# Loading the first feed-forward weights in two halves of 64 rows, with an activation tile between them

## The chip, the cores and the metric

One core of one Trainium2 chip. The metric is device time in microseconds (us) of one execution. Times inside a profile count from the start of its span, which is some 1.8 us shorter than the timed execution.

## The reference

The kernel computes a layer norm, then attention and a gated feed-forward network on the normalised input, and multiplies the two:

```python
x  = A_x                              # 1 x 2048 x 448, bf16
xn = layernorm(x)
s  = attention(xn, k_cache[last 512], v_cache[last 512], wq, wo)   # 16 heads of 256, 8 kv heads
g  = silu((gelu(xn @ w_gate) * (xn @ w_up)) @ w_down)              # w_gate, w_up: 448 x 1792
out = x + s * g
```

Only the first 10 us matter here. There the kernel loads x in tiles of 128 rows (called x0, x1, x2, x3 below), normalises and transposes them, and starts the gate and up products.

## The kernel before

The width 448 is three blocks of 128 rows of weights (k = 0, 1, 2) and a remainder of 64 rows. TensorE runs products of 64 rows in pairs, one on array rows 0 to 63, one on rows 64 to 127. In phase 0 the gate product takes the lower rows and the up product the upper ones; in phase 1 they change places.

```python
def group(units, lo, hi, start, stop, phases=(0, 1)):
    for p in phases:
        ph, part = p if isinstance(p, tuple) else (p, None)
        ks = {None: [2, 1, 0, NK], 0: [2, 1], 1: [0, NK]}[part]     # NK: the remainder rows, phase 0 only
        ...
            for u, j in ((0, ph), (1, 1 - ph)):                     # u: row half, j: 0 gate, 1 up
                rows = slice(R * u, R * u + R)                      # R = 64
        ...
        o = mms(lst, reads + rr + xb, b_ps[b:b + 2], before)        # waits for what it reads

load_x("sp", 0, 1)          # x0 on SyncE's queue (SP)
load_x("act", 1, 1)         # x1 on ScalarE's queue (ACT)
load_w("sp", 0, 0)          # gate, block 0: 128 rows x 3 k x 384 columns, 288 KB
load_w("act", 0, 1)         # up, block 0
load_x("sp", 2, 1)          # x2
load_wr("sp", 0, 0)         # remainder rows, 48 KB each
load_wr("act", 0, 1)
load_x("act", 3, 1)         # x3
...
act(tmp[:, 1, 0:1], epst[:, :], ACT.Sqrt, ...)   # brings ScalarE's table in, behind its four issues
load_x("sp", 4, 2)
for i in (1, 2):            # blocks 1 and 2, all on SP
    load_w("sp", i, 0); load_w("sp", i, 1); load_wr("sp", i, 0); load_wr("sp", i, 1)
```

The order of the engines' work in the head matters too. In every trace here VectorE and ScalarE run their instructions in the order in which the program lists them:

```python
ln_first(0); ln_first(1)              # statistics (VectorE), deviation (ScalarE)
ln_second(0)                          # reciprocal, normalise (VectorE)
ln_tp_pe(0, ((0, 6), (1, 4)))         # transposes on TensorE, copies on ScalarE
ln_second(1, "act")
ln_first(2)                           # statistics of x2: its deviation stands ahead of ...
gu_group(HEAD, PH, (0, 1), ((0, 0),)) # tile 0: phase 0, k = 2 and 1
ln_tp_pe(1, T)                        # ... the copy of the transposed tile 1 on ScalarE
gu_group(HEAD, PH, (0, 1), ((0, 1), 1))
ln_bn(3)                              # statistics of x3, ahead of tile 2's normalisation
ln_second(2)
ln_aggr(3); ln_std_act(3); ln_second(3)
gu_group(HEAD[:2], PH[:2], (1, 2), (0,))
ln_tp_pe(2, T)
...
```

The softmax here doesn't subtract the row's maximum and nothing guards it: scores larger than these inputs give would overflow.

## Time and profile before

| | before |
|---|---|
| time, first 3 runs | 556.67 us (556.21 to 556.74) |
| span of the profiled execution | 554.7 us |
| TensorE (PE) busy | 547.6 us, 99% |
| chain of waits on PE | 98% |

From the page of the kernel before: its first line, PE's busy time, and the chain that ended last.

```profile
span 554.7 us, 9719 instructions
PE 547.6 (99%) x3603; PEld 261.2 (47%) x3628; DVE 317.2 (57%) x817; ACT 273.6 (49%) x727; POOL 32.7 (6%) x64
...
PE 98%; DMA 1%; issue 0%; DVE 0%; SPq 0%; ACT 0%
```

The chain in order of time, kernel before (start us, us, what):

```profile
1.65 4.66 DMA x<-in_A_x_dram
6.34 0.64 DVE stats L375
7.00 0.19 DVE mv L378
7.22 0.29 ACT ve L391
7.51 0.49 ACT xnT L322
8.14 0.62 PE bank L328 x16
...
10.18 116.23 PE bank L328 x1028
```

The last thing that TensorE ever waits long for is x2: its load, its statistics, its deviation, and behind the deviation, on the same engine, a copy that belongs to tile 1. After 10.18 us the chain is matmuls almost to the end. The timeline of the same kernel (start us, us, engine, line, what, and in brackets the idle time before it and its releaser):

```profile
1.18 0.42 SPq L316 DMA_DIRECT2D wgu<-in_B_w_gate_dram  x1
1.65 0.48 SPq L316 DMA_DIRECT2D x<-in_A_x_dram  x1
2.89 1.28 ACT L322 ACT_TABLE_LOAD   x1 [2.89 <-issue]
6.34 0.63 DVE L375 BATCH_NORM_STATS2 stats<-x 128x6 f32<-128x448 bf16 x1 [0.30 <-DMA x<-in_A_x_dram]
8.14 0.34 PE L328 MATMUL bank<-xnT,wgu 64*128 64x128 bf16 x6 [0.37 <-ACT xnT L322]
```

When a load is complete is read below from the semaphore events in the trace: each load adds 16 increments, and the time of the last one is quoted.

### The profile page before, as it was taken

How to read it: one execution, taken by the hardware profiler on the slowest of the kernel's cores; microseconds unless marked ns; L12 is line 12 of the kernel's file. 1: busy time of each engine (PE TensorE's matmuls, PEld its weight loads, DVE VectorE, ACT ScalarE, POOL GpSimd, SP SyncE). 2: the span in 40 equal slices, each digit the busy share in tenths (PEclk: the TensorE clock that was granted, in tenths of full speed). 3: DMA queues.
4: the chain of work that ended last, by engine and by line, in shares of the span. 5: the costliest groups of instructions: out<-in, count | busy, mean ns of one | idle time of the engine just before them, and what ended most of it. 6: DMA issues, size and time to landing. Idle time of an engine off the chain costs nothing.

```text
span 554.7 us, 9719 instructions
## 1 busy us (share of the span) xinstructions
PE 547.6 (99%) x3603; PEld 261.2 (47%) x3628; DVE 317.2 (57%) x817; ACT 273.6 (49%) x727; POOL 32.7 (6%) x64
## 2 busy tenths in 40 slices
PE   8999999999999999999999999999999999999997
PEld 5554444444544444554444444544444454444455
DVE  6673734443385588326588745258747625858722
ACT  5432324353485588205588635058747505758600
POOL 1120580000000000000000000000000000000000
PEclk9999999999999999999999999999999999999999
DMA  9540399901156077413086803157704713618601
GB/s 295 115 141 9 79 302 307 213 1 39 38 134 96 5 149 157 88 35 92 1 153 152 153 1 77 33 94 164 146 11 95 134 34 90 153 19 153 153 8 34
DMA packets 163599, 57.63 MB, mean 104 GB/s; under 512 B 151456, under 2 KB 160672, under 8 KB 163552
## 3 DMA queue, kind: packets, MB, share of 16 engines
q1 hardware_dynamic: 159488, 45.16, 38.8%
q0 software_dynamic: 3296, 11.27, 6.7%
q8 instruction: 29, 0.48, 0.4%
q10 hardware_dynamic: 768, 0.57, 0.3%
q14 instruction: 18, 0.15, 0.1%
HBM read 17.92 MB, written 1.84 MB: 36 GB/s over the span
## 4 chain that ended last, share of the span: by engine, by line
PE 98%; DMA 1%; issue 0%; DVE 0%; SPq 0%; ACT 0%
PE bank L328 98%; DMA x<-in_A_x_dram 1%; SPq L316 0%; DVE stats L375 0%; ACT xnT L322 0%; DVE tmp L681 0%; ACT ve L391 0%; DVE ofin L684 0%; PE bank L426 0%; DVE mv L378 0%
## 5 line engine op out<-in xcount | busy, mean ns | idle before, releaser
L643 ACT ACTIVATE p<-bank 128x512 f32<-128x512 f32 x256 | 149.2, 597 | 103.3 <-PE bank L328 101.4
L647 DVE TENSOR_SCALAR pn<-p,rden 128x512 bf16<-128x512 f32 x256 | 124.6, 487 | 14.4 <-DMA pT<-pn 5.4
L328 PE MATMUL bank<-pT,va 128*128 128x512 bf16 x512 | 120.8, 379 | 0.0
L328 PE MATMUL bank<-kT,qT 128*128 128x512 bf16 x487 | 117.8, 379 | 2.0 <-ACT qT L322 1.0
L328 PE MATMUL bank<-wo,oT 128*128 128x448 bf16 (+2 forms) x544 | 97.7, 341 | 0.0
L328 PE MATMUL bank<-xnT,wq 64*128 64x512 bf16 x768 | 94.4, 376 | 0.0
L328 PE MATMUL bank<-xnT,wgu 64*128 64x512 bf16 (+2 forms) x768 | 83.9, 350 | 0.4 <-ACT xnT L322 0.4
L328 PEld LDWEIGHTS bank<-pT,va 128*128 128x128 bf16 x512 | 50.1, 98 | 60.4 <-DMA pT<-pn 0.2
L328 PEld LDWEIGHTS bank<-kT,qT 128*128 128x128 bf16 x512 | 49.6, 98 | 61.3 <-issue 2.5
L328 PEld LDWEIGHTS bank<-wo,oT 128*128 128x128 bf16 x544 | 52.0, 98 | 45.5
L630 DVE CAST qT<-bank 128x512 bf16<-128x512 f32 x64 | 42.9, 692 | 51.9 <-PE bank L328 51.9
L322 ACT ACTIVATE qT<-bank 128x512 bf16<-128x512 f32 x64 | 38.2, 597 | 60.7 <-PE bank L328 59.1
L328 PEld LDWEIGHTS bank<-xnT,wq 64*128 64x128 bf16 x768 | 36.9, 94 | 46.5 <-ACT p L643 2.1
L322 ACT ACTIVATE gl<-bank 128x512 bf16<-128x512 f32 x56 | 33.2, 597 | 49.4 <-PE bank L328 46.2
L494 DVE TENSOR_TENSOR actT<-bank,gl 128x512 bf16<-128x512 f32 x56 | 37.8, 689 | 33.4 <-PE bank L328 26.6
L328 PEld LDWEIGHTS bank<-xnT,wgu 64*128 64x128 bf16 x768 | 36.9, 94 | 37.4 <-issue 0.7
L643 ACT ACTIVATION_READ_ACCUMULATOR p<-bank 128x1 f32 x256 | 52.8, 206 | 0.0
L646 DVE RECIPROCAL rden<-rsum 128x1 f32<-128x1 f32 x256 | 40.4, 158 | 20.6 <-ACT p L643 20.0
L681 DVE SCALAR_TENSOR_TENSOR tmp<-bank,g 128x448 f32<-128x448 f32 (+2 forms) x17 | 10.1, 597 | 72.5 <-PE bank L328 72.5
L666 DVE CAST oT<-bank 128x512 bf16<-128x512 f32 x64 | 43.8, 684 | 6.9 <-PE bank L328 6.9
L328 PE MATMUL bank<-wd,actT 128*128 128x448 bf16 x224 | 43.0, 353 | 0.0
L322 ACT ACTIVATE oT<-bank 128x512 bf16<-128x512 f32 x64 | 39.1, 611 | 7.0 <-PE bank L328 7.0
(39 smaller groups left out, 182.9 us busy)
## 6 DMA issues: line engine op xcount, KB each, us to landing
wo<-in_A_wo_dram POOLq DMA_DIRECT2D x4, 896.0 KB, 19.0
wq<-in_A_wq_dram POOLq DMA_DIRECT2D x2, 1536.0 KB, 10.0
va<-in_A_v_cache_dram POOLq DMA_DIRECT2D x8, 256.0 KB, 13.9
pT<-pn SPq DMA_TRANSPOSE x128, 2.8
xr<-in_A_x_dram POOLq DMA_DIRECT2D x16, 112.0 KB, 2.3
out_dram<-ofin SPq DMA_DIRECT2D x15, 112.0 KB, 1.7
wd<-in_B_w_down_dram SPq DMA_DIRECT2D x1, 1568.0 KB, 7.6
x<-in_A_x_dram SPq DMA_DIRECT2D x2, 448.0 KB, 4.4
```

What stands on the lines that cost most here:

```text
L322: K.op("act", lambda e, o=o, i=i: e.activation(o, i, func, scale=scale), reads, writes)
L328: ins = e.matmul(o, lhsT=l, rhs=r, start=st, stop=sp)
L494: K.op("dve", lambda e: e.tensor_tensor(actT[:, c % 2, f, :], bank[b + 1], gl[:, s, :], ALU.mult), (b_ps[b + 1], b_gl[s]), (b_actT[c % 2][ ...
L630: K.op("dve", lambda v, s=s, b=b: v.tensor_copy(qT[:, s, 1, :], bank[b + 1]), (b_ps[b + 1],), (b_qT[s][1],))
L643: K.op("act", lambda e, b=b, r=r, z=z: e.activation(p32[:, z, :], bank[b], ACT.Exp, scale=att_scale, accum_out=rsum[:, r:r + 1]), (b_ps[b] ...
L646: K.op("dve", lambda e, r=r: e.reciprocal(rden[:, r:r + 1], rsum[:, r:r + 1]), (b_rsum[r],), (b_rden[r],))
L647: K.op("dve", lambda e, r=r, z=z, y=y, t=t4 % 2: e.tensor_scalar(pn[:, y, t, :], p32[:, z, :], rden[:, r:r + 1], None, op0=ALU.mult), (b_p ...
L666: K.op("dve", lambda v, i=i, b=b: v.tensor_copy(oT[:, i, :], bank[b]), (b_ps[b],), (b_oT[i],))
L681: K.op("dve", lambda e: e.scalar_tensor_tensor(out=tmp[:, s, c0:c1], in0=bank[b][:, c0:c1], scalar=0.5, in1=g2[:, t, c0:c1], op0=ALU.mult, ...
```

## The change

Phase 0 needs only the lower gate rows and the upper up rows. So these 144 KB each are loaded first, x2 and the remainder rows come next, and the other halves after them. Tile 0 is to start on half the weights, and x2 is to come 288 KB sooner. x3 moves from ScalarE's queue to SP's, so that ScalarE still issues four loads.

```diff
-        def load_w(q, i, j):
+        def load_w(q, i, j, half=None):
             w = (B_w_gate, B_w_up)[j]
             lo, hi = FBL[i] * P, FBL[i + 1] * P
-            dma(q, wgu[:, j, :, lo:hi], w[0:K3, lo:hi].rearrange("(k p) f -> p k f", p=P), (), (b_wl[i][j],))
+            rows = slice(0, P) if half is None else slice(R * half, R * half + R)
+            dma(q, wgu[rows, j, :, lo:hi], w[0:K3, lo:hi].rearrange("(k p) f -> p k f", p=P)[rows], (),
+                b_wl[i][j] if half is None else b_wl[i][j][half:half + 1])
 ...
-        load_w("sp", 0, 0)
-        load_w("act", 0, 1)
+        load_w("sp", 0, 0, 0)
+        load_w("act", 0, 1, 1)
         load_x("sp", 2, 1)
         load_wr("sp", 0, 0)
         load_wr("act", 0, 1)
-        load_x("act", 3, 1)
+        load_w("sp", 0, 0, 1)
+        load_w("act", 0, 1, 0)
+        load_x("sp", 3, 1)
 ...   (each product waits for the halves of its phase: reads -> reads[ph])
```

More of the change, by code (lines that the diff above doesn't have):

```diff
@@ L278, in bass_recurrent_scan__sliding_block_cached__geglu_ffn__prompt_kernel @@
         FBL = [0, 3, 6, 9, NF]
-        b_wl = [[K.buf() for j in range(2)] for i in range(4)]
+        b_wl = [[[K.buf() for u in range(2)] for j in range(2)] for i in range(4)]
         b_wlr = [[K.buf() for j in range(2)] for i in range(3)]
@@ L471, in group @@
                     rr = rreads if ph == 0 and NK in ks else []
-                    o = mms(lst, reads + rr + xb, b_ps[b:b + 2], before)
+                    o = mms(lst, reads[ph] + rr + xb, b_ps[b:b + 2], before)
                     last_row[b] = (o, ph)
@@ L483, in gu_group @@
                 units.append((b, lambda j, k, fc=fc: wgu[:, j, k, fc], wgur[:, fc], slice(c * QC + lo, c * QC + hi),
-                              b_wl[wi] + [b_wgu], b_wlr[min(wi, 2)], b_xnT[c * 4 + lo // P:c * 4 + hi // P]))
+                              [[b_wl[wi][0][ph], b_wl[wi][1][1 - ph], b_wgu] for ph in range(2)], b_wlr[min(wi, 2)], b_xnT[c * 4 + lo // P:c * 4 + hi // P]))
             group(units, lo, hi, lo == 0, hi == QC, phases)
@@ L623, in q_group @@
             units = [(b, lambda j, k, i=i: wq[:, k, (h + i) * Dh + j * P:(h + i) * Dh + (j + 1) * P],
-                      wqr[:, h + i, :], slice(c * QC, (c + 1) * QC), b_wql[h // HG][:1], b_wql[h // HG][1:], b_xnT[c * 4:c * 4 + 4])
+                      wqr[:, h + i, :], slice(c * QC, (c + 1) * QC), [b_wql[h // HG][:1]] * 2, b_wql[h // HG][1:], b_xnT[c * 4:c * 4 + 4])
                      for i, b in enumerate(pairs)]
```

## The prediction

> **What bounds the kernel.** TensorE. The page gives PE 547.6 us of a 554.7 us span (99%), and the chain of waits gives PE 98%. From 10.18 us to the end that chain is matmuls with gaps of 0.05 to 0.30 us, so a change to the first loads can only act in the first 10 us. There the chain runs: x tile 2 in flight until 6.34, its statistics on VectorE (0.64), aggregate (0.19), deviation on ScalarE (start 7.22, 0.29), then on ScalarE, in order behind it, the copy of the transposed tile 1 (start 7.42), then PE at 8.14. PE's last matmul of tile 0 ends at 7.77: a hole of 0.37 us. The transposes of tile 1 were done at 6.90 (timeline), so the copy waited 0.5 us for something it does not read.
>
> **What changes.** No compute instruction is added; the bytes are the same. The first gate and up loads (288 KB each) become four halves of 64 rows; x tile 3 moves from ACT's queue to SP's, so SP has two more issues (0.4 to 0.6 us each) and its later loads are issued about 1.1 us later. Tile 0's phase 0 waits for 288 KB of weights rather than 576, and x tile 2 has 288 KB fewer before it.
>
> **Costs from the trace.** Semaphores of before: gate weights complete at 5.26, up at 5.74, x2 6.32, remainder rows 6.29 and 6.50, x3 6.69. DMA runs at about 370 GB/s from 4 us on, at 170 to 250 before. 288 KB are 0.8 to 1.2 us: I estimate x2 at 5.1 to 5.5, remainder rows about 5.5, second halves 6.0 to 6.6, x3 6.4 to 6.9. The Trainium skill, "DMA: Bandwidth & Descriptors", section Issuing engines are not separate DMA queues, says that loads issued by several engines run on the same 16 DMA engines and interleave; the overlapping landings here agree. So halves give no bandwidth, only order.
>
> **What is on the path.** VectorE cannot use x2 before about 6.0: it normalises tile 1 until 6.04, and its wait before x2's statistics is just 0.30 us. So a landing 1 us earlier is worth only 0.30 to 0.36: statistics at 6.0, deviation at 6.88, copy at 7.08, PE at about 7.8, joining tile 0's last matmul. Everything to 10.18 moves by about 0.35, if x3 lands by about 6.75 (its statistics follow directly) and the second halves by 7.0 (phase 1 starts at 7.09). Later weights have about 1 us to spare: block 1 landed at 9.25 and is first used after 11. After 10.18 nothing is gained or given back: PE is saturated.
>
> **Prediction.** 556.67 - 0.35 = 556.3 us, range 555.8 to 556.7. The three runs of before spread by 0.53 us, more than the gain. Faster by over 2%: 0.5%; within 2%: 99%; slower: 0.5%.
>
> **In the profile.** Right if VectorE's wait for x before tile 2 goes from 0.30 to 0, the PE hole at 7.77 to 8.14 falls below 0.1, the first matmul of 512 columns (12.34) comes at about 12.0, and PE is otherwise unchanged. The chain then passes through VectorE's work on tiles 0 and 1.
>
> **What would make it wrong.** Halves of 64 rows moving slower than whole loads, so that phase 1 waits at 7.1 (loss up to 0.5); x3, now sixth on SP, landing after 7.0 and delaying tiles 2 and 3; longer issues on ScalarE, which delay its table load (2.89 to 4.17) and tile 0's whole chain by 0.1 to 0.2 us; the hole coming back at tile 2's or 3's copy.

## The result

The changed kernel took 557.25 us (median of 6, 557.06 to 558.5) where before took 556.44 (median of 6, 556.06 to 558.27). The ratio is 1.0013, 95% interval 0.9997 to 1.0029. The same kernel was timed twice more: 1.0019 (1.0006 to 1.0031) and 1.0020 (1.0007 to 1.0032). The first interval takes in 1, those of the two repeats do not. The changed kernel is slower by about 1 us (0.81, 1.10 and 1.03 between the medians), a fifth of a per cent, where 0.35 us less was predicted; and it lies outside the predicted range.

The page of the changed kernel:

```profile
span 556.7 us, 9747 instructions
PE 550.1 (99%) x3628; PEld 261.1 (47%) x3628; DVE 317.1 (57%) x817; ACT 273.8 (49%) x727; POOL 32.7 (6%) x64
...
PE 97%; DMA 2%; SPq 1%; DVE 0%; issue 0%
```

Its chain in order of time:

```profile
1.18 0.73 SPq L316
...
1.96 0.83 SPq L316
...
3.36 0.75 SPq L316
...
4.15 4.77 DMA x<-in_A_x_dram
8.95 0.63 DVE stats L379
...
9.67 0.62 DVE xn L405 x2
...
10.34 0.29 PE bank L430 x8
...
11.93 274.78 PE bank L328 x1958
286.70 4.83 DMA pT<-pn
```

The chain now starts with SP's issues, waits for an x tile up to 8.92 us, and enters the unbroken stretch of matmuls at 11.93 in place of 10.18. The x tile is now x3, not x2. The timeline:

```profile
1.18 0.73 SPq L316 DMA_DIRECT2D wgu<-in_B_w_gate_dram  x1
1.96 0.83 SPq L316 DMA_DIRECT2D x<-in_A_x_dram  x1
3.21 1.28 ACT L322 ACT_TABLE_LOAD   x1 [3.21 <-issue]
6.22 0.63 DVE L379 BATCH_NORM_STATS2 stats<-x 128x6 f32<-128x448 bf16 x1
8.35 0.85 PE L328 MATMUL bank<-xnT,wgu 64*128 64x128 bf16 x24 [0.90 <-PE bank L328]
8.95 0.63 DVE L379 BATCH_NORM_STATS2 stats<-x 128x6 f32<-128x448 bf16 x1 [1.88 <-DMA x<-in_A_x_dram]
10.34 0.29 PE L430 MATMUL bank<-ident,xn 64*128 64x64 bf16 x8 [0.86 <-DVE xn L405]
```

What was predicted did happen at 6.22: VectorE no longer waits for x2 (nor in the second profile; in the third it waits 0.19 us). But a half of the gate weights now takes 0.73 us to issue where the whole took 0.42. ScalarE's table load is 0.32 us later. Phase 1 of tile 0 waits to 8.35. And VectorE waits 1.88 us for x3. The releaser named at 8.35, "PE bank", cannot be the real one: TensorE had been idle for 0.90 us. That product also waits for the second halves, and the last event of the second gate half is at 8.25 us.

Last semaphore event of each load, us; three profiles of each kernel (first, second, third):

| load | before | changed |
|---|---|---|
| gate, whole / first half | 5.26, 5.11, 5.32 | 5.71, 5.65, 5.96 |
| up, whole / first half | 5.74, 5.91, 5.54 | 5.52, 5.33, 5.78 |
| x2 | 6.32, 6.21, 5.86 | 6.20, 6.13, 6.40 |
| gate remainder rows | 6.50, 6.59, 6.19 | 6.79, 6.66, 6.97 |
| up, second half | | 6.88, 7.05, 6.89 |
| gate, second half | | 8.25, 7.58, 7.41 |
| x3 | 6.69, 6.77, 6.47 | 8.92, 7.76, 8.26 |

Half of the gate weights arrives later than all of them did, and x2, with 288 KB fewer ahead of it, at about the same time.

### The profile page after: what moved, and what is told of

Its sections match the earlier page's. It is cut to its first block, busy times and chain, and to the rows that moved or that the text cites. A ratio compares the mean times of both kernels' runs of the same rounds, so it can differ in the third digit from the quotient of the medians.

```text
span 556.7 us, 9747 instructions
## 1 busy us (share of the span) xinstructions
PE 550.1 (99%) x3628; PEld 261.1 (47%) x3628; DVE 317.1 (57%) x817; ACT 273.8 (49%) x727; POOL 32.7 (6%) x64
## 4 chain that ended last, share of the span: by engine, by line
PE 97%; DMA 2%; SPq 1%; DVE 0%; issue 0%
PE bank L328 97%; DMA pT<-pn 1%; DMA x<-in_A_x_dram 1%; SPq L316 1%; DVE stats L379 0%; DVE xn L405 0%; PE bank L430 0%; DVE tmp L685 0%; DVE ofin L688 0%; DVE rstd L399 0%
## 5 line engine op out<-in xcount | busy, mean ns | idle before, releaser
L328 PE MATMUL bank<-kT,qT 128*128 128x512 bf16 x512 | 121.0, 379 | 0.0
```

Of the source, the lines that this page charges most:

```text
L328: ins = e.matmul(o, lhsT=l, rhs=r, start=st, stop=sp)
```

## The experiments

The theories. A: loads of 64 rows move slower than whole ones, and their lateness is the loss. B: the first profile was a disturbed execution. C: x3's place at the end of SP's queue is the loss. D: more loads in another order cost, whatever their rows.

A table that serves all experiments. TensorE's weight loads were matched one by one with those of the first profile of before; the difference in start (us, negative is earlier) at tile 0's transposes (5.38 in before), at 23.3 us and at the end:

| kernel | tile 0's transposes | 23.3 us | end | median time, before of the same rounds |
|---|---|---|---|---|
| before_again | -0.04 | -0.11 | +0.14 | 556.43, 556.25 |
| before_third | +0.03 | -0.05 | -0.05 | 556.44 (1 run), 556.23 |
| changed, first profile | +0.19 | +1.74 | +1.99 | 557.25, 556.44 |
| after_again | +0.20 | +0.58 | +0.92 | 557.21, 556.11 |
| after_third | +0.19 | +1.08 | +1.38 | 557.23, 556.20 |
| x3_back | +0.84 | +1.52 | +1.52 | 558.08, 556.11 |
| together | +0.20 | +0.88 | +1.01 | 557.31, 556.25 |
| even_odd | +0.24 | +0.82 | +0.82 | 557.36 (1 run), 556.25 |
| gate_only | -0.06 | -0.11 | +0.29 | 557.00, 556.23 |
| bn3_later | +0.20 | +0.40 | +0.60 | 556.90, 556.20 |
| k_split | -0.06 | -0.05 | -0.04 | 556.62, 556.11 |
| k_split_again | -0.03 | -0.41 | -0.41 | 556.13 (1 run), 556.20 |
| x2_first | +0.05 | -0.35 | -0.35 | 556.23, 556.11 |
| x2_first_again | -0.06 | -0.32 | -0.31 | 556.32, 556.23 |
| x2_first_x3_sp | +0.11 | -0.29 | -0.29 | 556.39, 556.23 |
| late_halves | -0.03 | -0.20 | -0.20 | 556.15 (1 run), 556.25 |
| late_k | +0.01 | -0.28 | -0.01 | 556.34 (1 run), 556.20 |

What is gained or lost in the head stays to the end nearly to the hundredth, save for a few later gaps of 0.1 to 0.4 us. One caution: the zero of this table, the first profile of before, is the slowest of the five whose first loads are those of before (with before_again, before_third, late_halves and late_k); the other four are 0.05 to 0.28 ahead of it at 23.3 us.

### The changed kernel again

No edit.

> The changed kernel once more, to learn which of its first profile is the kernel and which the occasion. Theory A (loads of 64 rows move slower): again +0.5 to +1.3 us over before; second gate half and x3 complete after 7.0 again, with packets of 768 bytes taking over 0.1 us after 5 us from the start. Theory B (the first profile, at 558.5, was a disturbed execution): +-0.3 us of before, x3 complete by 7.0.

557.21 against 556.11, ratio 1.0019 (1.0006 to 1.0031); second gate half at 7.58, x3 at 7.76. As A expected, but for its slow packets: those of 768 bytes took 36 to 49 ns on average in each half-microsecond from 5 to 10.5 us, not over 0.1 us. B falls. The first profile, however, was a bad instance: its second gate half and x3 were 0.7 and 1.2 us later than here.

### x3 back on ScalarE's queue

```diff
         load_w("act", 0, 1, 0)
-        load_x("sp", 3, 1)
+        load_x("act", 3, 1)
```

> The change with x tile 3 put back on ScalarE's queue, halves kept. Theory A (64 rows are slow): the second gate half still completes after 7.0, the time stays within 0.3 us of the changed kernel. Rival C (the loss is x3 standing sixth on SP's queue): x3 completes before 7.0 and the time is 0.5 to 1 us below the changed kernel, at or below before.

558.08 us, ratio 1.0034 (1.0021 to 1.0046): 0.9 us above the changed kernel. C falls (x3 still came at 7.91, and last on SP's queue behind whole rows, in k_split below, it came at 6.68), and A's number missed too, for a reason that neither named. From its chain:

```profile
3.87 1.28 ACT L322
...
6.23 0.50 PE bank L430 x8
```

ScalarE must finish its issues before it brings its table in. The table load starts at 2.89 behind four whole issues, at 3.21 behind the four of the changed kernel (two of them halves), and at 3.87 behind five; and tile 0's transposes go from 5.38 to 5.58 to 6.23. So the change's move of x3 to SP was needed, and a slow issue on ScalarE costs compute as well. In this profile TensorE also reached its full clock late (the trace's record of it begins at 9.71 us, against 4.88 in before), so not all of its 1.52 us is the table load.

### x2 first, all loads whole

```diff
+        load_x("sp", 2, 1)
         load_w("sp", 0, 0)
         load_w("act", 0, 1)
-        load_x("sp", 2, 1)
```

> The kernel before with one line moved: x tile 2 ahead of the gate weights on SP, all loads of 128 rows. It gives the early x2 without halves and without another issue. If the mechanism I predicted (x2's landing costs TensorE 0.35 us) is right: VectorE's wait for x2 gone, the hole before tile 1 gone, 0.25 to 0.4 us below before, gate weights complete at about 5.6. If x2 was not what TensorE waited for: within 0.1 us of before.

The head did what was predicted for x2:

```profile
6.00 0.62 DVE L375 BATCH_NORM_STATS2 stats<-x 128x6 f32<-128x448 bf16 x1
7.08 0.58 ACT L322 ACTIVATE xnT<-bank 128x512 bf16<-128x512 bf16 x1
```

VectorE's wait is gone, the copy of tile 1 starts at 7.08, as the prediction put it, and TensorE is 0.35 us ahead from there to the end of the profiled execution. The timed runs do not show it: 556.23 against 556.11, ratio 1.0003 (0.9989 to 1.0016). So that gain stands in this profile, measured from the slowest profile of before, and is unseen in the timing.

### The first weights cut by k, not by rows

```diff
-            rows = slice(0, P) if half is None else slice(R * half, R * half + R)
-            dma(q, wgu[rows, j, :, lo:hi], w[0:K3, lo:hi].rearrange("(k p) f -> p k f", p=P)[rows], (),
+            ks = slice(0, NK) if half is None else (slice(1, NK), slice(0, 1))[half]
+            dma(q, wgu[:, j, ks, lo:hi], w[0:K3, lo:hi].rearrange("(k p) f -> p k f", p=P)[:, ks], (),
 ...   (tile 0's products with k = 2, 1 wait for the first pieces only, all others for both)
```

> The change with the first weights cut by k (k=1,2 then k=0; 192 and 96 KB, all 128 rows) in place of by rows; same number and order of loads. Theory A (64 rows are slow): second pieces complete by 6.6, x3 by 6.9, the time 0.2 to 0.4 us below before. Rival D (two more issues and the order cost it, whatever the rows): second pieces after 7.0, 0.5 us or more above before, like the changed kernel.

Same number of loads, same order, same queues as the change, same bytes; only the pieces differ: 192 and 96 KB of all 128 rows. First pieces at 4.37 and 4.80, x2 at 5.37, second pieces at 5.96 and 5.76, x3 at 6.68. For the landings D falls: neither two more loads nor the order made these pieces, x2 and x3 late in the changed kernel. Behind them the cut by k was not free: from 5.5 to 6.5 us the DMA engines moved 133 GB/s (125 in the repeat, 366 in before), x4 and x5 came at 8.22 (7.23 in before) and block 1 was complete at 10.48 (9.24). Nobody waited for those, since block 1 is first used after 11 us. TensorE was 0.45 us ahead of before until 14.3 us, where the next product started 0.4 us late (0.23 us of it idle), with no wait in the profile, and the lead was lost. Time 556.62, ratio 1.0008 (0.9996 to 1.0021), so A's time was missed, and D's, 0.5 us or more above before, was met by the medians (0.51), though the interval takes in 1. It is 0.6 us below the changed kernel of the same rounds. Whether the gap belongs to the kernel was open.

### Before, profiled again

No edit, twice.

> The kernel before, profiled once more and timed against itself. Its 15 timed runs so far fall into two groups, most at 556.0 to 556.3, some at 556.5 to 556.7, and the first profile (556.48) is of the upper group. Theory E (the hole before tile 1 is there only in some executions, so an early x2 has little to win): a profile at about 556.1 shows x2 complete by about 6.0 and PE's tile 1 at about 7.8. Rival F (the hole is always there, and x2_first's gain of 0.35 in the head was lost to chance): PE's tile 1 at 8.1 again, x2 complete at 6.3. Ratio 1.000 within 0.0006.

> A third profile of the kernel before. Theory E (the hole before tile 1 varies from execution to execution with x2's landing): x2 completes between 5.8 and 6.4 and the start of tile 1 on TensorE follows it, between 7.8 and 8.15, so the time is 556.1 if early and 556.5 or more if late. Rival F (always there): x2 at 6.2 to 6.3 and tile 1 at 8.0 to 8.15 with a time of 556.1.

The second profile: 556.59 us, x2 at 6.21, tile 1 on TensorE at 8.04 after a hole of 0.31 us. The third: 556.44, x2 at 5.86, so VectorE did not wait; yet tile 1 was no earlier, for tile 0's first twelve products, which took 0.56 us in the first profile, took 0.80. The trace's record of TensorE's full clock begins at 4.88 us in the first profile and at 7.05 in the third; before it, pairs of these products start 0.08 to 0.11 us apart, after it mostly 0.05 to 0.07. E, that an early x2 alone makes a fast run, is not borne out; F as stated is not either. Three profiles of before stand at 556.44 to 556.59 while more than half of the timed runs lie at 556.0 to 556.3, so the profiled executions are not quite the timed ones.

### Alternate rows

```diff
-            rows = slice(0, P) if half is None else slice(R * half, R * half + R)
+            rows = slice(0, P) if half is None else slice(half, P, 2)
 ...   (every product waits for all four pieces)
```

> The change with the 64 rows of a half taken alternately (even rows, then odd rows, over all 128 partitions), every product waiting for all four pieces; results stay right, TensorE starts late on purpose. Theory A1 (64 rows in one half of the partitions are slow): the issues of the pieces take 0.45 us as whole loads do, all four complete by 6.3. Theory A2 (any load of 64 rows by 3 pieces is slow, where ever they lie): issues of 0.7 us, pieces of 144 KB complete at 7.0 to 8.3 as in the changed kernel.

Issues of 0.75, 0.73, 0.74 and 0.64 us; second gate piece at 7.47, x3 at 7.73. The same slowness with rows spread over all 128 partitions: A2, not A1. In the issues and the second pieces, which rows the half takes makes no difference that this one profile shows. Its first pieces (5.34 and 5.13) and x2 (5.70) came earlier than in the three profiles of the change; so they did in x3_back (5.31, 5.08 and 5.81), which has the change's halves.

### Halves late, where the queue is full

The first loads as in before; blocks 1 and 2 in halves of rows, on SP alone:

```diff
-            load_w("sp", i, 0)
-            load_w("sp", i, 1)
+            load_w("sp", i, 0, 0)
+            load_w("sp", i, 1, 1)
+            load_w("sp", i, 0, 1)
+            load_w("sp", i, 1, 0)
```

> The first loads as in the kernel before; the weights of blocks 1 and 2 in halves of 64 rows, on SP alone, in the stretch where whole loads ran at 370 GB/s. The cost of the half by itself. Theory A: issues of 0.7 us against 0.47 to 0.59, DMA throughput in 6.5 to 9 us falls to 200 to 300 GB/s, block 1 complete 1.5 us or more later than 9.25. If halves cost only in the first microseconds (queues starting up): 350 GB/s or more, block 1 complete by 9.7.

And its control, the same count and mean size of pieces, cut by k:

> late_halves with blocks 1 and 2 cut by k (192 and 96 KB, all 128 rows) in place of rows (144 KB of 64 rows): same count, same order. If the 64 rows cost: issues of 0.41 to 0.59, throughput between 6.5 and 8.5 us of 300 GB/s or more, packets of 768 bytes at about 36 ns. If it is the smaller pieces: throughput of 215 to 310 GB/s and packets of 45 to 65 ns, as in late_halves.

Busy time by engine in the stretch from 6.5 to 8.0 us, for before, late_halves and late_k in this order; the last two columns are the DMA engines' busy share and GB/s:

```profile
core 0: us, PE busy (x) PEld busy (x) DVE busy (x) ACT busy (x) POOL busy (x), PEclk, DMA share, GB/s
6.50:8.00 1.50, 1.27 (x42) 1.01 (x38) 1.43 (x5) 0.78 (x2) 0.00 (x0) 1.00 1.10 369
```

```profile
6.50:8.00 1.50, 1.50 (x52) 1.41 (x50) 1.43 (x7) 0.89 (x2) 0.00 (x0) 1.00 1.12 260
```

```profile
6.50:8.00 1.50, 1.50 (x59) 1.42 (x57) 1.43 (x7) 0.80 (x3) 0.00 (x0) 1.00 1.09 365
```

Halves of rows move 260 GB/s where whole loads move 369 and pieces cut by k move 365, with the DMA engines just as busy. From 6.5 to 8.5 us, the stretch named for late_k beforehand, it is 260, 369 and 329: late_k too slows down after 8 us. A packet of 768 bytes took 43 to 63 ns on average in the three half-microseconds to 8.0 of late_halves and 36 ns in the other two. The issues took 0.61 to 0.66 us for the halves and 0.43 to 0.59 for the pieces by k (seven of eight at most 0.47). The second piece, 144 KB in late_halves and then 192 KB in late_k:

```profile
4.09 0.61 SPq L316 DMA_DIRECT2D wgu<-in_B_w_up_dram  x1
```

```profile
3.90 0.47 SPq L316 DMA_DIRECT2D wgu<-in_B_w_up_dram  x1
```

At 144 KB in each issue of 0.61 us and the 0.04 us between, SP alone cannot feed more than 147456 / 0.65 = 227 GB/s (an estimate from these numbers). So it is the 64 rows, not the size or the number of pieces, and not the first microseconds. Each of the two is one profile. A's sizes were too large: block 1 was complete at 9.87, 0.63 us later than in before and not 1.5 (9.10 in late_k). The time of late_halves, 556.15, is not above before: block 1 is first used after 11 us.

### Both halves side by side

```diff
         load_w("sp", 0, 0, 0)
         load_w("act", 0, 1, 1)
+        load_w("sp", 0, 0, 1)
+        load_w("act", 0, 1, 0)
         load_x("sp", 2, 1)
         load_wr("sp", 0, 0)
         load_wr("act", 0, 1)
-        load_w("sp", 0, 0, 1)
-        load_w("act", 0, 1, 0)
```

> The change with x tile 2 and the remainder rows put back behind both halves: halves of 64 rows, no new order. If halves are slow, all that follows is slower still than in the changed kernel: x2 complete after 6.8 (6.32 before), time 0.3 us or more above the changed kernel. If it is the new order or x3's place that costs, not the halves: x2 at 6.3 to 6.5 and the time at or below the changed kernel.

x2 at 7.21, 0.9 us later than in the first profile of before, with the same bytes ahead of it (and its own issue at 2.85 in place of 1.65): the cost of the halves without the order. The time, 557.31 (ratio 1.0015, 1.0000 to 1.0031), is that of the changed kernel, not 0.3 above it. So the order of the change does bring x2 forward, by about 1 us; the halves take that much away first.

### x2 first, repeated, and with x3 on SP

> x2_first once more, since its 5 runs did not show the 0.35 us that its profile gained in the head. Under E most of its runs lie at 556.1 and the median within 0.2 of before (whose better half lies there too); the profile again has tile 1 at 7.77. Under F it lies 0.25 to 0.4 below before.

```diff
-        load_x("act", 3, 1)
+        load_x("sp", 3, 1)
```

> x2_first with x tile 3 moved to SP as in the change: three issues on ScalarE in place of four, all loads whole. If ScalarE's issues set the start of tile 0 through the table load (theory of the loss: +0.36 us at the table load gave +0.20 at tile 0's transposes), one issue less puts the table load at 2.3 in place of 2.85 and tile 0's transposes 0.1 to 0.25 us before 5.38; time 0.1 to 0.3 below before, the best so far. If the start does not depend on it: transposes at 5.38 to 5.44 again, time as x2_first.

Ahead by 0.32 and 0.29 us in the profiles, and 556.32 and 556.39 against 556.23 in the timing: ratios 1.0008 (0.9994 to 1.0023) and 1.0001 (0.9989 to 1.0014). With one issue fewer the table load came at 2.21, but tile 0's transposes at 5.49: x0 and x1 came at 3.37 and 3.53 here, and they set the start. So at 2.85 the table load was not what held the start; at 3.21 it was. No version that beats before in timed runs was found; what x2 seems worth, at most 0.3 us, is a twentieth of a per cent, and the intervals reach two to three times that to either side.

### Only the gate weights in halves

```diff
-        load_w("act", 0, 1, 1)
+        load_w("act", 0, 1)
 ...
-        load_w("act", 0, 1, 0)
-        load_x("sp", 3, 1)
+        load_x("act", 3, 1)
```

> The change with only the gate weights in halves; the up weights whole and x tile 3 on ScalarE, as before. It takes apart the two ways in which halves cost. ScalarE's issues are those of before, so its table load is at 2.9 and tile 0's transposes at 5.38 (5.58 in the changed kernel). What is left is the slow landing on SP: second gate half after 6.8, x2 no earlier than 5.7; loss over before 0 to 0.5, under half of the changed kernel's. If the loss stays at 0.8 to 1.1, the delayed table load was not a part of it.

With ScalarE's issues whole, the table load is at 2.85 and tile 0's transposes at 5.33, as expected. The second gate half came at 7.33 and x2 at 6.21; x3 at 6.54, and TensorE was 0.11 us ahead of before at 23.3 us. Then at 289 us a wait for a DMA transpose cost 0.4 us:

```profile
289.87 1.90 PE L328 MATMUL bank<-pT,va 128*128 128x512 bf16 x8 [0.22 <-DMA pT<-pn]
```

That wait is also in one of three profiles of before, in all three of the changed kernel (0.08 to 0.34 us of shift that stays), in bn3_later and in together, and not in the others. Timed, gate_only lies at 557.00, ratio 1.0012 (0.9999 to 1.0025): more than half of the changed kernel's loss, against the expectation. Its profile and its time do not agree, so how the loss divides between ScalarE and SP is not settled by it.

### Tile 3's statistics behind tile 2's normalisation

```diff
-        ln_bn(3)
         ln_second(2)
+        ln_bn(3)
         ln_aggr(3)
```

> The changed kernel with VectorE's statistics of tile 3 moved behind the normalisation of tile 2, so that a late x3 no longer holds tile 2 up. If x3's landing (7.8 to 8.9) is what TensorE pays for through VectorE's order: tile 2's transposes at about 8.7 in place of 9.2, time 0.3 to 0.6 us below the changed kernel. If TensorE pays for the second gate half and the late table load alone: within 0.15 us of the changed kernel.

> The changed kernel in the same rounds, for the comparison: 0.8 to 1.1 us above before, second gate half complete after 7.0, x3 after 7.6.

556.90 against 557.23 for the changed kernel in the same rounds. In the changed kernel, tile 2's transposes waited for VectorE, which waited for x3 (8.26):

```profile
9.67 0.29 PE L430 MATMUL bank<-ident,xn 64*128 64x64 bf16 x8 [0.82 <-DVE xn L405]
```

In bn3_later they start on time (before: 8.59), and the wait shows up again one step further on:

```profile
8.58 0.29 PE L430 MATMUL bank<-ident,xn 64*128 64x64 bf16 x8
...
9.10 0.29 ACT L395 ACTIVATE ve<-mv,epst 128x1 f32<-128x1 f32 x1 [1.14 <-DVE mv L382]
9.30 0.58 ACT L322 ACTIVATE xnT<-bank 128x512 bf16<-128x512 bf16 x1
...
10.02 0.34 PE L328 MATMUL bank<-xnT,wgu 64*128 64x128 bf16 x6 [0.41 <-ACT xnT L322]
```

Now ScalarE holds the copy of tile 2 back behind the deviation of tile 3. So about a third of the loss in these rounds was x3 through VectorE's order (the ranges of the two kernels, 556.77 to 557.31 and 557.14 to 557.90, still touch), and of what is left a part is the same x3 through ScalarE's order.

### The cut by k, once more

No edit.

> The cut by k once more. If what took its 0.45 us back belongs to it: TensorE again 0.4 us ahead of before up to 13 us and again loses 0.3 to 0.4 at about 14.3 us. If that was chance: no such gap, span about 554.2.

TensorE 0.41 us ahead, from tile 1 to the end, span 554.3, no gap at 14.3: that gap is not in every execution. The single timed run, 556.13, lies among the fast half of before; the five of k_split, 556.46 to 556.99, do not, so how often the gap comes, and whether the cut by k gains anything, stays open.

## Why the prediction was wrong

The step that failed is "So halves give no bandwidth, only order." Halves of 64 rows took bandwidth and issue time away: 260 GB/s in place of 369 where the queue was full, and 0.73 us to issue in place of 0.42. The prediction's last paragraph named slow halves, a late x3 and the late table load as what would make it wrong, so they were foreseen but counted in neither the sum nor the range. Term by term:

- **Issue of a half**: put at 0.4 to 0.6 us, measured 0.73 and 0.75 on SP and 0.70 and 0.62 on ScalarE, in every profile of the change. x2's own issue behind a half went from 0.48 to 0.83. SP's later loads were issued not 1.1 us later but 1.87 (block 1's first issue 3.40, now 5.27).
- **x2's landing**: put at 5.1 to 5.5, measured 6.13 to 6.40 (5.81 in x3_back). The 288 KB fewer ahead were worth the predicted microsecond (together against the change), but the halves cost as much. Cut by k, x2 landed at 5.37 and 5.51, inside the range.
- **Second halves**: put at 6.0 to 6.6, measured 6.88 to 8.25. Tile 0's phase 1 waited 0.90 us for them in the first profile and under 0.2 in the other two.
- **x3**: put at 6.4 to 6.9, measured 7.76 to 8.92. This is the late landing with the longest reach: from tile 1's first product to tile 2's transposes TensorE's delay against before grew from 0.68 to 1.80, from 0.09 to 0.64 and from 0.08 to 1.13 us in the three profiles. It goes through two in-order queues: VectorE's statistics of tile 3 ahead of tile 2's normalisation, then ScalarE's deviation of tile 3 ahead of tile 2's copy.
- **ScalarE's table load**: named as a risk of 0.1 to 0.2 us and not counted; it came 0.32 us later and cost 0.20 at tile 0.
- **Right**: the bound (TensorE after 10 us; what the head loses stays to the end, save for the later gaps), and that VectorE's own work caps the worth of an early x2. x2's wait on VectorE did vanish in the first profile; another wait took its place.
- **Not settled**: how much an early x2 is worth. 0.30 to 0.36 was predicted; against the first profile of before the three profiles with whole loads and x2 first are 0.29 to 0.35 ahead and the two cut by k 0.41 and 0.45 (before later gaps). But the mean of the five profiles with before's first loads is itself 0.13 ahead of that first one, which leaves the three 0.19 (an estimate from the table), and the timed runs show no gain.

The Trainium skill, "DMA: Bandwidth & Descriptors", Rules for kernel authors, advises against two transfers to disjoint partition halves, "Use one 128-partition transfer", because they share the same engines. The advice held here, and had it been weighed, the range could have reached above 557. Its reason, that they serialise, does not seem enough: the pieces by k, loaded one behind the other on the same queue, moved 365 GB/s, and the halves 260.

What stays open: why a load of 64 rows by three pieces is slow. Not by its side of the partitions (even_odd), its size or count (late_k), the start-up (late_halves) or its neighbours (together). Loads of 64 rows by one piece, as those of the remainder rows, were not tested by themselves. Each half still showed 16 separate semaphore events, spread over 0.6 to 2.1 us, so it was not confined to fewer of the 16 engines; that 64 rows divide over 16 is what the same page's section Why a DMA increments its semaphore by 16 and not by 1 says too. Open as well is how the 1 us of the timed loss divides: k_split, with the same order and count of loads, has 0.5 of it by the medians of its five runs and none in the single run of its repeat. And that the 0.3 us in the profiles of x2_first is not in its timed runs is in part the choice of a slow profile as zero; whether the rest is real these intervals do not tell.

## What to carry to other kernels

If a first load must be split so that work can start on a part of it, cut it along the free dimension and keep all 128 rows: the same split with full rows landed every piece on time, though it made no timed gain here and the loads behind it came about 1 us later. Count the issue time of each piece on the engine that issues it, above all where that engine has work behind it, such as a table load. And when an order is changed, follow every tile that moved back through the in-order queues: a load that nobody waits for today may stand ahead of something that everybody waits for.

## What the Trainium skill lacked or had wrong

- "DMA: Bandwidth & Descriptors", Rules for kernel authors: the row on two halves of the partitions says that they serialise, and gives neither a rate nor an issue time. Halves of 64 rows by three pieces ran at 260 GB/s (6.5 to 8.0 us) beside 369 for whole loads and 365 for pieces of the same mean size with 128 rows, and took 0.61 to 0.75 us to issue beside 0.41 to 0.59.
- The same page, Issuing engines are not separate DMA queues, calls the time to initiate a DMA usually small relative to the DMA itself. Here an issue of 0.73 us stands against 0.4 us that 144 KB would take at the 370 GB/s of these traces (an estimate), and two issues of halves among ScalarE's four put its table load 0.32 us later.
- No page gives the issue time as it depends on the rows; even and odd rows cost the same as upper and lower ones (0.75 and 0.73 us).
- "TensorE: Matmul & The Clock Gate", Part 1, puts the moment at which TensorE reaches full speed around 4 us into sustained matmuls, give or take 0.5 us from run to run. That it varies agrees; the spread was larger here. In the three profiles of before the trace's record of the full clock begins at 4.88, 5.37 and 7.05 us, which is 3.7, 4.2 and 5.9 us after the first matmul, and tile 0's first twelve products took 0.56, 0.56 and 0.80 us. (The window view prints a clock of 1.00 even before that, where the record holds nothing.) In the third profile tile 0 ended 0.4 us later, more than the change was to win.
